# A delta-rule attention kernel with a gated MLP: scaling and turning in one operation, later joins, moves on ScalarE's queue

## The chip, the cores and the metric

One core of a Trainium2 chip runs one program: a linear attention with the delta rule, then a two-layer MLP with SiLU. The metric is the device time in microseconds. The kernel before took 643.09 us, the median of three runs (639.18 to 647.69).

## The reference

The inputs are q, k, v of shape (4 batches, 8 heads, 768 tokens, 48) in float32, beta of shape (4, 8, 768), and two weight matrices of 384 x 2048 and 2048 x 384.

```python
k_n = k / (np.linalg.norm(k, axis=-1, keepdims=True) + 1e-06)
state = np.zeros((B, H, D, D))
for t in range(S):
    y[:, :, t] = np.einsum('bhd,bhde->bhe', q[:, :, t], state)
    v_old = np.einsum('bhde,bhd->bhe', state, kt)
    state = state + bt * np.einsum('bhd,bhe->bhde', kt, vt - v_old)
x = y.transpose(0, 2, 1, 3).reshape(3072, 384)
h = x @ w_in
out = (h * (1.0 / (1.0 + np.exp(-h)))) @ w_out
```

## The kernel before

The 768 tokens are cut into six chunks of 128 (numbered 0 to 5), each chunk into two halves of 64 tokens, each half into two blocks of 32. Batches 0 and 1 form group 0 (`G0`), batches 2 and 3 group 1 (`G1`). Inside a chunk the recurrence over tokens is a unit triangular system for each of the 32 (batch, head) pairs. The kernel inverts it, and then needs the running `state` only at the borders of halves.

The stages for one chunk `c`, with the names that the profile shows:

- **Norms.** `lengths(c)` squares the keys (`square`, L409 to L426: tile `sq`, or `z` for chunks above 2, where the room of `z` is borrowed), sums them (`add_squares`, L427, tile `ss`) and runs `norm_steps` (L435): some twenty tiny VectorE operations that end in `spread` (the scale of each row, which feeds the matmul `pg` and its copy `step`) and `n_slot`, by which GpSimd scales the values `vf` (`size`, L521).
- **Scores.** `prepare(c)` turns the last keys and queries with VectorE's stream transpose (`turn_all`, L542, tile `kq`) and multiplies keys by keys and queries for each of the four batches (`score`, matmuls `pa` at L583). For each batch ScalarE copies one product out (`ap<-pa`, L598) and VectorE masks the other (L593). The PSUM room `A` has three banks that are handed out in turn; in this stretch the order of users is `pyc` of group 0, `pyc` of group 1, `pg`, then `pa` of batches 0, 1, 2, 3. So batch 2's scores take the bank of `pg` and wait for ScalarE's copy `step<-pg` (L504), and batch 3's take batch 0's bank and wait for its copies and masks. The 32 x 32 diagonal blocks go through DRAM (`blocks<-ap`, `g<-blocks`) so that each partition holds one block.
- **Inversion.** `invert(c)` (L678) does 31 steps of two VectorE operations each (`rank`, L689, and `x`, L694). It then scales `x` by `step` (L697), turns the lower rows' blocks into `g` (`turn_rows`: a quarter by GpSimd, L604, three quarters by VectorE, L601), and sends `g` and `x` through DRAM (`low<-g`, `up<-x`) to come back transposed as `xe`, `xi` and `crosses`.
- **Joins.** `merge` (L828, matmuls `py` and `px` at L843) joins blocks of 32 to triangles of 64. The first of them needs `xe<-low`.
- **Solve.** `solve(c)` takes the joins, then for each half: `keys` (`ph`, L889, which VectorE adds to `vf` at L894), `inner` (`pz`, L901, copied by ScalarE to `z`), `old` and `new` (`pyc`, L969 and L982) and `update` (`pu`, L921, added to `state` at L928). `even_heads` writes the half's outputs into `xT`, the MLP's transposed input. ScalarE copies the odd heads to `part` first, then copies twelve strips of even heads into `xT`. The odd heads cross partitions by five DMAs, `xT<-part`, issued by `move`.
- **MLP.** `feed_forward(c)`: chunk 1 uses plain products (`hidden`, `phid`, L1110), chunks 2 to 5 use seven products in place of eight (`hidden_by_products`, `hx` and `hu`, L1164, with sums of weights made once by `sum_w_in`, L1140, and sums of inputs made by `sum_x`, L1152). `combine` (`px` and `py`, L1330) does the second layer in the same way; ScalarE and VectorE collect its pieces (`o` at L1368 to L1374, `kept` at L1338, `o<-o,kept` at L1341).

**What sets the order.** `pin` fixes the order of instructions on each compute engine as the program issues them. `in_line` does the same for DMAs of SyncE's queue. A DMA on that queue waits for its data in place, and those behind it wait too. `linked` and `deep(..., n)` add waits: with `deep` and n = 3 each DMA of a load waits until the third one before it has landed. `run(n)` issues n pieces of the MLP of the chunk before (a piece is a handful of matmuls), and the main loop mixes pieces with stages of the chunk in hand: `go(steps, n)` advances a generator by n steps. So the MLP's matmuls are the filler that TensorE runs while a chunk's chain is with other engines. `paced` spreads the inversion of chunks 3 to 5 over the 44 items of `hidden_by_products`. Chunk 2's inversion is spread by a credit (L1800 to L1809), and four more pieces are run between its end and its joins (L1816).

`load_blocks(src, c, bs)` brings a group's keys or queries of a chunk in 32-row blocks, by six DMAs. Its rooms are the MLP's `gT`, or `ap`, or (for chunk 2) rooms of weight sums. The room `ap` takes first G0's keys and then G1's queries, so the latter wait until VectorE has turned the former.

Of the kernel before, what the change touches and what calls it, by code (L numbers as in the profile page):

```python
# [19 lines left out]
def kernel(  # L20
# [388 lines left out]
    def square(c, b):  # L409
# [12 lines left out]
        if (c, b) == (0, 3):  # L422
            pin(nc.scalar.activation(out=squared[c, b], in_=kb, func=ACTF.Square))
        else:
            pin(nc.gpsimd.tensor_tensor(out=squared[c, b], in0=kb, in1=kb, op=ALU.mult))
# [252 lines left out]
    def invert(c, step):  # L678
# [3 lines left out]
        def turn_rows(engine, s):  # L682
            engine(g[EVEN, :, s], x[EVEN, s, :].rearrange("p s t -> p t s"))

        for m in range(T - 1, 0, -1):
# [11 lines left out]
        pin(nc.vector.tensor_tensor(  # L697
            out=x, in0=x, in1=step[:].unsqueeze(2).to_broadcast([P, T, T]), op=ALU.mult
        ))
        for _ in range(1):  # L700
            yield
        if c == 1:
            put_up(x)
            return
        turn_rows(by_pool, slice(0, T // 4))
        turn_rows(by_dve, slice(T // 4, T))
        low, up = (tc.dram_tile([n, T, T], FP32, name=f"{name}{c}") for name, n in (("low", W), ("up", P)))
        issue(low[:], g[EVEN])
        issue(up[:], x)
# [250 lines left out]
    def move():  # L960
        for to, of in moves:
            in_line(nc.sync.dma_start(out=to, in_=of))
        moves.clear()
# [60 lines left out]
    def made(c, hf):  # L1024

        together(update(c, 0, hf), update(c, 1, hf))
        together(new(c, 0, hf), new(c, 1, hf))
        move()
        copy_out()
# [7 lines left out]
    def solve(c):  # L1037
# [34 lines left out]
        for hf in range(2):  # L1072
# [14 lines left out]
            copy_out()  # L1087
            if hf == 0:
                yield
# [712 lines left out]
    while left:  # L1802
        spent[0] = 0.0
        run()
        credit += 1.31 - spent[0]
        while left and credit > 0.0:
            left = next(steps, 0) != 0
            credit -= 0.38 + 0.00225 * m * (T - m) if m > 0 else 1.2
            m -= 1  # L1809
        if m == T - 6:  # L1810
            load_k(3)
    deep(load_blocks, k, 3, G1, n=3)
# [3 lines left out]
    for n in range(4):  # L1816
        run()
        go(after, (1, 1, 1, 0)[n])

    for c in range(2, NCH):  # L1820
        solving, more = solve(c), c + 1 < NCH
        for n in range(8):
            go(solving)
            run((1, 1, 2, 2, 1, 1, 2, 2)[n] if c == 2 else (2, 2, 2, 2, 1, 1, 2, 2)[n])
            if n == 2 and c > 2 and more:
                assert done[0] >= start(c) - OUTPUT - 4
                deep(load_blocks, k, c + 1, G1, n=3)
            if n == (1 if c == 2 else 3) and more:
                deep(load_blocks, q, c + 1, G0, n=3)
            if n > 2:  # L1830
                go(after, 8)
            if n == 5 and c == 2:
                go(sums_in, 2)
# [10 lines left out]
        go(prepare(c + 1))  # L1844
        linked(load_v, c + 1)
# [42 lines left out]
```

## Time and profile before

| | |
|---|---|
| Times of three runs | 643.09, 647.69, 639.18 us |
| The profiled execution's own time | 644.67 us |
| Its span, first to last instruction | 642.9 us (the rest, 1.8 us, lies around it) |
| Mean granted TensorE clock | 0.978 |
| TensorE busy | 615.2 us |
| VectorE / ScalarE / GpSimd busy | 445.9 / 239.2 / 100.5 us |
| DMA moved | 55.06 MB, mean 86 GB/s |

TensorE is busy or waiting; its idle time is 27.7 us in all (642.9 less 615.2). About 11.2 us of that lie in the first 180 us, where chunks 0 and 1 are begun, and 3.6 us at the end, after the last matmul. A row of the timeline has the start, the length, the engine, line and operation, out<-in with shapes, the count of merged instructions, and in brackets the idle time of the engine before it and what ended that. The profile counts two matmuls for each one of the program, since float32 takes two. A row with an engine's name and a "q" (SPq, ACTq) is the sequencer of that engine issuing a DMA.

### The profile page before, as it was taken

Reading aid. Unit: us, or ns where it says so; the run is one execution under the profiler, and the core shown is the slowest. Engines: PE = TensorE matmul, PEld = TensorE weight load, DVE = VectorE, ACT = ScalarE, POOL = GpSimd, SP = SyncE. Lnnn points to the kernel's source line nnn. Section 1 sums busy time; section 2 is a strip of 40 time slices with the busy share of each in tenths; the row PEclk is TensorE's granted clock in tenths of the full one; section 3 lists DMA queues with packets and bytes.
Section 4 is the critical chain, followed back from the end, with each engine's and each line's share of the span. In section 5 each row is a group of like instructions: output and inputs, shape, how many; then the busy total and the mean of one; then the engine's idle time right before and its main releaser. Section 6 shows DMA issues by size and latency. Waiting matters only on the chain.

```text
span 642.9 us, 21912 instructions
## 1 busy us (share of the span) xinstructions
PE 615.2 (96%) x9570; PEld 538.5 (84%) x9570; DVE 445.9 (69%) x946; ACT 239.2 (37%) x542; POOL 100.5 (16%) x99
## 2 busy tenths in 40 slices
PE   8889999999989969999999999999999999999997
PEld 5677788666779948898898988898998899988997
DVE  5855879998897953969884959895969965131332
ACT  3665665152251113434322434324434314434211
POOL 5442531245000040000050000050000020000000
PEclk9968999999999979999999999999999999999999
DMA  7755654165326166235073436074441060110011
GB/s 153 181 120 166 187 130 99 57 164 131 86 47 131 27 113 126 64 80 118 0 141 76 108 79 123 1 145 91 100 98 44 1 108 16 39 26 0 1 26 24
DMA packets 143935, 55.06 MB, mean 86 GB/s; under 512 B 113488, under 2 KB 137296, under 8 KB 143840
## 3 DMA queue, kind: packets, MB, share of 16 engines
q1 hardware_dynamic: 143360, 53.00, 37.1%
q8 instruction: 75, 1.23, 0.9%
q10 hardware_dynamic: 480, 0.67, 0.4%
q14 instruction: 20, 0.16, 0.1%
HBM read 40.99 MB, written 10.49 MB: 80 GB/s over the span
## 4 chain that ended last, share of the span: by engine, by line
PE 78%; DVE 10%; DMA 7%; issue 2%; SPq 1%; ACT 1%; POOL 1%; DVEq 0%; POOLq 0%
PE hu L1164 12%; PE px L1330 11%; PE hx L1164 10%; PE phid L1110 10%; PE py L1330 10%; PE po L1253 7%; PE pa L583 3%; PE pz L901 2%; DVE rank L689 2%; DVE x L694 2%; PE ph L889 1%; PE pyc L969 1%; DMA gT<-in_k_dram 1%; PE pu L921 1%; DMA gT<-in_q_dram 1%
## 5 line engine op out<-in xcount | busy, mean ns | idle before, releaser
L1110 PE MATMUL phid<-xT,w_in 128*128 128x256 f32 x384 | 92.6, 394 | 0.8 <-issue 0.7
L1110 PEld LDWEIGHTS phid<-xT,w_in 128*128 128x128 f32 x384 | 72.4, 194 | 12.0 <-issue 1.6
L1330 PE MATMUL py<-w_out,sums_of_g 128*128 128x192 f32 x320 | 57.6, 329 | 1.7 <-issue 1.5
L1330 PE MATMUL px<-sums_of_w,sums_of_g 128*128 128x192 f32 x320 | 56.8, 328 | 0.0
L1330 PEld LDWEIGHTS py<-w_out,sums_of_g 128*128 128x128 f32 x320 | 52.2, 190 | 2.7 <-issue 2.1
L689 DVE SCALAR_TENSOR_TENSOR rank<-g,step,x 128x31 f32<-128x31 f32 (+15 forms) x124 | 49.6, 400 | 5.9 <-DMA g<-blocks 3.0
L1330 PEld LDWEIGHTS px<-sums_of_w,sums_of_g 128*128 128x128 f32 x320 | 52.3, 190 | 0.5
L1310 DVE TENSOR_TENSOR sums_of_g<-gT 128x512 f32<-128x512 f32 (+2 forms) x44 | 33.5, 797 | 25.0 <-PE py L1330 18.8
L1164 PE MATMUL hx<-xT,w_in 128*128 128x256 f32 x192 | 48.0, 379 | 0.0
L694 DVE TENSOR_TENSOR x<-x,rank 128x31 f32<-128x31 f32 (+15 forms) x124 | 42.5, 342 | 4.4
L1164 PE MATMUL hu<-xT,w_in 128*128 128x256 f32 x192 | 45.4, 379 | 0.0
L1179 DVE TENSOR_TENSOR gT<-gT,hx 128x512 f32<-128x512 f32 x32 | 21.9, 685 | 31.4 <-PE hx L1164 30.7
L1341 DVE TENSOR_TENSOR o<-o,kept 128x192 f32<-128x192 f32 (+1 forms) x29 | 12.4, 427 | 42.2 <-ACT kept L1338 42.2
L1164 PEld LDWEIGHTS hu<-xT,w_in 128*128 128x128 f32 x192 | 36.5, 190 | 5.0
L1164 PEld LDWEIGHTS hx<-xT,w_in 128*128 128x128 f32 x192 | 36.4, 190 | 4.8
L604 POOL COPY g<-x 64x256 f32<-64x256 f32 x4 | 5.0, 1255 | 179.7 <-DVE x L697 179.7
L598 ACT COPY xT<-pyc 48x128 f32<-48x128 f32 (+2 forms) x120 | 31.1, 259 | 1.6
L928 DVE TENSOR_TENSOR state<-state,pu 48x384 f32<-48x384 f32 x44 | 24.2, 551 | 9.1 <-PE pu L921 8.1
L598 ACT COPY gT<-hu 128x512 f32<-128x512 f32 x32 | 18.7, 585 | 30.6 <-PE hu L1164 30.6
L901 PEld LDWEIGHTS pz<-vf,xi 64*64 64x64 f32 x768 | 25.5, 142 | 4.9 <-DVE vf L894 2.4
L1164 PE MATMUL hu<-sums_of_g,w_in 128*128 128x256 f32 x128 | 28.9, 379 | 0.0
L901 PE MATMUL pz<-vf,xi 64*64 64x48 f32 x768 | 27.4, 226 | 1.5 <-DVE vf L894 1.5
(234 smaller groups left out, 1203.9 us busy)
## 6 DMA issues: line engine op xcount, KB each, us to landing
vf<-in_v_dram SPq DMA_DIRECT2D x48, 96.0 KB, 2.8
out_dram<-o SPq DMA_DIRECT2D x42, 96.0 KB, 2.2
w_out<-in_moe_w_in_dram SPq DMA_DIRECT2D x12, 256.0 KB, 3.4
sums_of_w<-in_moe_w_out_dram SPq DMA_DIRECT2D x8, 384.0 KB, 3.7
blocks<-ap SPq DMA_DIRECT2D x40, 64.0 KB, 1.9
g<-blocks SPq DMA_DIRECT2D x4, 512.0 KB, 3.5
up<-x SPq DMA_DIRECT2D x4, 512.0 KB, 4.2
xi<-up SPq DMA_DIRECT2D x16, 128.0 KB, 3.7
```

Of the source, the lines that this page charges most:

```text
L583: pin(nc.tensor.matmul(pa[e][half, p * n * W : (p + 1) * n * W], lhsT=kq[rows, p, 0, half], rhs=kq[rows, p, js[0] : js[-1] + 1, half], sta ...
L598: return pin(nc.scalar.copy(to, of))
L689: pin(nc.vector.scalar_tensor_tensor(out=tv, in0=g[:, 0:m, m : m + 1].to_broadcast([P, m, n]), scalar=step[:, m : m + 1], in1=x[:, m : m + ...
L694: yield pin(nc.vector.tensor_tensor(out=x[:, 0:m, m:T], in0=x[:, 0:m, m:T], in1=tv, op=ALU.add))
L901: yield pin(nc.tensor.matmul(pz[rows, n * D : (n + 1) * D], lhsT=xis[g][rows, u * H + 2 * p + e, :], rhs=vfs[c][rows, hf, g * HB + u, p, : ...
L928: pin(nc.vector.tensor_tensor(out=to, in0=to, in1=by_heads(pu[of]), op=ALU.add))
L1110: pin(nc.tensor.matmul(ph[:, j * GT : (j + 1) * GT], lhsT=w_in[:, a, (2 * f + j) * P : (2 * f + j + 1) * P], rhs=xTs[c, hf][:, a, :], star ...
L1164: pin(nc.tensor.matmul(to[:, GT * i : GT * (i + 1)], lhsT=weights[:, f], rhs=moving, start=start and i == 0, stop=True, skip_group_check=True,
L1179: return lambda: pin(nc.vector.tensor_tensor(out=at(fs, j, hf), in0=at(fs, j, hf), in1=of(room), op=ALU.add))
L1253: pin(nc.tensor.matmul(pos[i][:, 0:DM], lhsT=hidden_of(0, hf, f // 2)[:, at : at + C], rhs=w_outs[f // HFF][:, f % HFF, :], start=(f == 0) ...
L1310: pin(nc.vector.tensor_tensor(out=sums_of_g[:, k, fs], in0=of[0], in1=of[1], op=op))
L1330: pin(nc.tensor.matmul(to, lhsT=at, rhs=quarter(f, *b) if isinstance(b, tuple) else sums_of_w[b][:, f], start=start and n == 0, stop=n == ...
```

## The change

Six things change. In the inversion of chunks 2 to 5 the lower rows are scaled and turned by one VectorE operation that writes `g` in transposed order; then the whole of `x` is scaled in place. The separate turn by GpSimd and VectorE goes. After chunk 2's inversion seven runs of pieces stand in place of four before the joins. One step of the generator goes too, and the credit takes nothing for the last step, so the joins stand six matmuls of the program (12 records) of `phid` later in TensorE's order. The odd heads' DMAs of chunks 2 to 5 are issued by ScalarE, after the second group's even heads, and leave SyncE's queue. The squares for chunks 3 to 5 are made by ScalarE in place of GpSimd. The steps of `lengths` for chunk 3 (and by their order those for 4 and 5) are issued earlier in the solve, ahead of the state's update. The last steps of `sum_w_in` come after chunk 3's scores. The loads of key and query blocks that ran under `deep` run without it, and the queries of chunks 4 and 5 for G0 are issued one stage later.

```diff
-        if (c, b) == (0, 3):
+        if c > 2 or (c, b) == (0, 3):
             pin(nc.scalar.activation(out=squared[c, b], in_=kb, func=ACTF.Square))
...
-        def turn_rows(engine, s):
-            engine(g[EVEN, :, s], x[EVEN, s, :].rearrange("p s t -> p t s"))
-
...
-        pin(nc.vector.tensor_tensor(
-            out=x, in0=x, in1=step[:].unsqueeze(2).to_broadcast([P, T, T]), op=ALU.mult
-        ))
-        for _ in range(1):
+        def scale(rows, to):
+            pin(nc.vector.tensor_tensor(
+                out=to, in0=x[rows], in1=step[rows].unsqueeze(2).to_broadcast([rows.stop - rows.start, T, T]),
+                op=ALU.mult,
+            ))
+
+        if c == 1:
+            scale(ALL_ROWS, x)
             yield
-        if c == 1:
             put_up(x)
             return
-        turn_rows(by_pool, slice(0, T // 4))
-        turn_rows(by_dve, slice(T // 4, T))
+        scale(EVEN, g[EVEN].rearrange("p t s -> p s t"))
         issue(low[:], g[EVEN])
+        scale(ALL_ROWS, x)
         issue(up[:], x)
...
-    def move():
+    def move(by_scalar=False):
         for to, of in moves:
-            in_line(nc.sync.dma_start(out=to, in_=of))
+            issue(to, of, by_scalar)
...
         together(new(c, 0, hf), new(c, 1, hf))
-        move()
+        if c == 1:
+            move()
         copy_out()
...
             copy_out()
+            move(True)
...
-            credit -= 0.38 + 0.00225 * m * (T - m) if m > 0 else 1.2
+            credit -= 0.38 + 0.00225 * m * (T - m) if m > 0 else 0.0
...
-    deep(load_blocks, k, 3, G1, n=3)
+    load_blocks(k, 3, G1)
...
-    for n in range(4):
+    for n in range(7):
         run()
-        go(after, (1, 1, 1, 0)[n])
+        go(after, int(n < 3))
...
-                deep(load_blocks, k, c + 1, G1, n=3)
-            if n == (1 if c == 2 else 3) and more:
-                deep(load_blocks, q, c + 1, G0, n=3)
-            if n > 2:
+                load_blocks(k, c + 1, G1)
+            if n == (1 if c == 2 else 4) and more:
+                load_blocks(q, c + 1, G0)
+            if n > 0:
                 go(after, 8)
-            if n == 5 and c == 2:
-                go(sums_in, 2)
...
         go(prepare(c + 1))
+        go(sums_in)
+        go(sums_in)
```

In the order of the built programs the following stands around chunk 2's scores. ScalarE, before: six strips, `o<-px`, `step<-pg`, eight copies `ap<-pa`. After: six strips, five DMAs `xT<-part`, `kept<-py`, `step<-pg`, eight copies `ap<-pa`. VectorE, before: `kq<-ap` (batches 2 and 3), eight masks. After: `o<-o,kept`, then `kq<-ap`, eight masks. Around chunk 3's and 4's scores only the five DMAs are new, between the last strip and `o<-px`, `step<-pg`.

## The prediction

> **What bounds the kernel now.** I read the page first, for who is busy and what the chain of waits is made of.
>
> ```profile
> span 642.9 us, 21912 instructions
> ...
> PE 615.2 (96%) x9570; PEld 538.5 (84%) x9570; DVE 445.9 (69%) x946; ACT 239.2 (37%) x542; POOL 100.5 (16%) x99
> ...
> PE 78%; DVE 10%; DMA 7%; issue 2%; SPq 1%; ACT 1%; POOL 1%; DVEq 0%; POOLq 0%
> ```
>
> TensorE is the bound, and the change leaves its matmuls alone. It can only gain where TensorE stands still, and lose where it makes TensorE stand still. So next I went through TensorE's timeline for idle time after chunk 1, where the change acts.
>
> ```profile
> 235.02 0.32 PE L843 MATMUL py<-xe,ap 32*32 32x32 f32 x4 [5.31 <-DMA xe<-low]
> 236.17 1.92 PE L843 MATMUL py<-xe,ap 32*32 32x32 f32 x124 [0.83 <-DMA xe<-low]
> 238.01 2.93 PE L1110 MATMUL phid<-xT,w_in 128*128 128x256 f32 x6
> ...
> 263.19 0.25 PE L901 MATMUL pz<-vf,xi 64*64 64x48 f32 x1 [1.02 <-DVE vf L894]
> ...
> 372.91 1.10 PE L583 MATMUL pa<-kq 48*64 48x128 f32 x32 [1.21 <-DVE kq L542]
> 374.27 1.43 PE L583 MATMUL pa<-kq 48*64 48x128 f32 x32 [0.26 <-DVE ap L593]
> ...
> 453.72 0.25 PE L901 MATMUL pz<-vf,xi 64*64 64x48 f32 x1 [0.47 <-DVE vf L894]
> ...
> 521.54 1.25 PE L843 MATMUL py<-xe,ap 32*32 32x32 f32 x124 [0.31 <-DMA xe<-low]
> ```
>
> The brackets are the prize: 5.31 + 0.83 = 6.14 us at chunk 2's joins, 1.02 + 0.47 us for `vf`, 1.47 us at chunk 3's scores, 0.31 us at chunk 5's joins, 9.4 us in all. The third view is the granted clock (PEclk, behind the engines' columns) in windows of time.
>
> ```profile
> 54.90:58.30 3.40, 3.40 (x12) 2.73 (x11) 0.00 (x0) 1.87 (x3) 1.84 (x1) 0.50 0.38 131
> 177.70:181.20 3.50, 2.27 (x39) 1.81 (x37) 3.43 (x6) 3.35 (x13) 0.00 (x0) 1.00 0.12 31
> 235.00:242.60 7.60, 6.75 (x198) 5.54 (x198) 3.27 (x6) 1.75 (x3) 0.41 (x1) 0.50 0.84 128
> ```
>
> After the wait at the joins TensorE runs at half clock for 7.6 us. The 124 `py` take 1.92 us there against 1.25 us at chunk 5.
>
> **Part by part.** First the joins. The chain of waits shows the path into them, and what six records of `phid` cost at full clock.
>
> ```profile
> 226.71 1.24 DVE x L697
> 228.06 1.25 POOL g L604
> 229.32 3.33 DMA low<-g
> 233.09 3.03 DMA xe<-low
> ...
> 240.94 1.84 PE ph L889 x64
> ...
> 245.50 2.79 PE phid L1110 x12
> ...
> 525.59 1.16 PE ph L889 x63
> ```
>
> The scaled turn does in one step of VectorE what L697 and L604 do in two, so `low` leaves at about 227.97 in place of 229.32, 1.35 us sooner. I cost the new step, 64x1024 with a transposed write, like L697, which has as many elements per partition (1.24 us). The turn that it replaces is the nearest row for the access pattern:
>
> ```profile
> 227.97 0.84 DVE L601 COPY g<-x 64x768 f32<-64x768 f32 x1
> ```
>
> Scaled to 1024 elements that is 1.12 us, with the stride on the reading side; no row has it on the writing side. I keep from 1.12 to twice 1.24 us. The Trainium skill, "SBUF — State Buffer", "Door 1: The DMA port swizzle", says that an access which crosses into a new 16-byte line each time pays a penalty, which speaks against this step; row L601 reads in such strides and pays none, and writing is shown by no run here. The scaling of `x` for `up` comes 1.24 us behind, so `up` leaves at about 229.25 against 229.8: nothing lost.
>
> TensorE gets 12 more records of `phid` before the joins, 2.79 us. Idle time left: 6.14 − 1.35 − 2.79 = 2.00 us, so 4.14 us are gained. The 12 records are missing later, between chunk 2's scores and its products, where nothing waits for TensorE to be slow. Half clock cost 0.67 us on `py`, 1.53 us on `phid` (2.93 against half of 2.79) and 0.7 us on `ph` (1.84 against 1.16), 2.9 us together. Whether it goes is open: the window at 177.7 us, with 1.2 us of idle time in it, kept the clock at 1.00, but at 54.9 us the clock was lost without a long wait. I take half, 1.4 us, with 0 and 2.9 as ends. The other three inversions save the same 1.35 us; only chunk 5's joins wait, so 0.31 us there.
>
> Norms sooner: VectorE's queue around 263.19.
>
> ```profile
> 254.65 2.30 DVE L928 TENSOR_TENSOR state<-state,pu 48x384 f32<-48x384 f32 x4 [5.91 <-PE pu L921]
> ...
> 261.27 1.28 DVE L1140 TENSOR_TENSOR w_in<-w_in 128x512 f32<-128x512 f32 x2
> 262.58 1.02 DVE L894 TENSOR_TENSOR vf<-vf,ph 128x384 f32<-128x384 f32 x2
> ```
>
> Between `state` and `vf` stand 5.6 us of norms and sums. They move into the 5.91 us of idle time before `state` or behind the scores, so `vf` comes when `ph` does, and 1.02 us go; in chunk 4 0.47 us go the same way. Sum 1.5 us, between 0.5 and 2.
>
> Squares on ScalarE: the kernel has one already.
>
> ```profile
> 8.69 0.52 ACT L423 ACTIVATE sq<-gT 128x384 f32<-128x384 f32 x1 [0.27 <-DMA gT<-in_k_dram]
> ```
>
> Four of these for each of three chunks stand beside TensorE's filler. I cost them at nothing: ScalarE is idle 63% of the span. Were that cover gone, the price would be 2.1 us a chunk. Loads without `deep` and a shorter SyncE queue let G1's queries land sooner, which would end chunk 3's 1.47 us. They can also crowd the `xi` transfers after the joins; I bound that by 0 to 1 us and take 0.
>
> Now what the DMAs on ScalarE's queue cost.
>
> ```profile
> L962 SPq DMA_DIRECT2D xT<-part x55: 597/607/1432, 89.5 to 557.1; - x55
> ...
> 91.64 0.37 ACTq L102 DMA_DIRECT2D g<-blocks  x1
> 92.06 0.60 ACT L1118 ACTIVATE gT<-phid 128x512 f32<-128x512 f32 x1 [0.92 <-DMA xT<-part]
> ```
>
> An issue holds SyncE's sequencer for 0.61 us, so five take 3.0 us, 3.2 us with the gaps. Row 91.64 shows that ScalarE computes nothing while its sequencer issues. The DMAs read `part`, which is written before the strips, so some of the issuing can run while the last strips are still being worked off: ScalarE stands still for between 0 and 3.2 us. I take 2.2 us, as the only row of such an issue has it wholly exposed. What is queued behind it, in chunk 2:
>
> ```profile
> 272.99 1.61 ACT L598 COPY xT<-pyc 48x128 f32<-48x128 f32 x6
> 274.63 0.33 ACT L1374 ACTIVATE o<-px 128x192 f32<-128x192 f32 x1
> ...
> 272.88 2.04 DVE L542 STREAM_TRANSPOSE kq<-ap 128x512 f32<-128x512 f32 x2
> 275.55 3.38 DVE L593 TENSOR_TENSOR ap<-pa,above 128x256 f32<-128x256 f32 x8 [0.62 <-ACT ap L598]
> 280.91 0.36 DVE L1341 TENSOR_TENSOR o<-o,kept 128x192 f32<-128x192 f32 x1 [0.72 <-ACT kept L1338]
> ...
> 273.99 3.72 PE L583 MATMUL pa<-kq 48*64 48x128 f32 x128
> ```
>
> Behind it stand `kept<-py`, then `step<-pg` (whose bank batch 2's scores take), and on VectorE `o<-o,kept` ahead of `kq<-ap`. The strips end at 274.6, the DMAs at 276.8, `kept` at 277.15, `o` (0.36) at 277.5, the first `kq` (1.02) at 278.6. Batch 2's scores, ready at 273.99 + 1.86 = 275.85, wait 2.8 us. Batch 3's wait for masks behind the second `kq`, 0.5 to 1 us. Sum 3.8 us; with nothing exposed 1.6 us are left by VectorE's new order, with 3.2 us exposed 4.8 us. Chunks 3, 4 and 5:
>
> ```profile
> 367.29 3.25 ACT L598 COPY xT<-pyc 48x128 f32<-48x128 f32 x12
> ...
> 463.52 1.61 ACT L598 COPY xT<-pyc 48x128 f32<-48x128 f32 x6
> 464.52 4.05 PE L583 MATMUL pa<-kq 48*64 48x128 f32 x128
> ...
> 557.75 0.33 ACT L1374 ACTIVATE o<-px 128x192 f32<-128x192 f32 x1
> 559.48 2.76 PE L1330 MATMUL px<-sums_of_w,sums_of_g 128*128 128x192 f32 x16
> ```
>
> In chunk 4 `step` ends at 465.13 + 2.2 + 0.5 = 467.85, and batch 2's scores, ready at 466.55, wait 1.3 us. In chunk 3 the strips end at 370.54, so `step` ends at 373.25, where batch 2 began at 372.91, so the 1.47 us are not gained but change hands: 0. In chunk 5 `o<-px` ends at 560.25, and the `px` of 559.48 that adds to what it reads waits 0.75 us.
>
> **The sum.** −4.14 − 1.4 − 0.31 − 1.5 + 3.8 + 1.3 + 0 + 0.75 = −1.5 us. The profiled execution took 644.67 us (642.9 and 1.8 around it); that gives 643.2 us, and on the median of 643.09 us, 1.6 us below it, **641.5 us**. What is gained at the joins is given back at the scores. Own range of this case, with the ends of the clock, of the exposure and a run's noise: 637 to 647.
>
> **Rivals.** *The issue is hidden* (nearly all of it runs while strips are worked off). Then the scores cost 1.6 us, chunk 3's 1.47 us are gained, and the clock stays up: −4.14 − 2.9 − 0.31 − 2 − 1.47 + 1.6 = −9.2 us, 634 us. For it: `part` is long written when the strips end. Against it: the exposed issue of row 91.64.
>
> *ScalarE's queue becomes the bound at the scores.* If all 3.2 us are exposed, the waits are 4.8, 1.0, 2.3 and 1.75 us, 9.9 us in place of 5.85. A wait of 3 to 4 us in the middle of small `pa` matmuls then halves the clock as at 235 us, where it was low for 10.2 us (7.6 us, and 2.6 us before it); dense work loses half of that, 5.1 us a time. One such loss gives 643.09 − 1.5 + 4.0 + 5.1 = 650.7 us, two 655.8. It decides from some 2.5 us of wait on. For it: 5.31 us idle lost the clock. Against it: the window at 177.7 us, where a wait of 1.2 us lost nothing. The Trainium skill, "TensorE: Matmul & The Clock Gate", Part 1, says that one idle window of about 3.4 us halves the clock; by that rule chunk 2's 2.8 us would just not, and the row at 54.9 us, lost without so long a pause, says that less can do.
>
> *The strided write costs double* (2.5 us). `low` leaves no sooner, and the joins gain only 2.79 us: 643.2 us.
>
> **Chances.** Forecast 0.5, issue hidden 0.2, ScalarE's queue 0.2, strided write 0.1. The range 633 to 651 reaches to the hidden issue and to one loss of clock. Two per cent is 12.9 us, about what a measurement of this kernel can tell from no change. To be faster by that, the hidden issue would need nearly every bracket above and more: 0.07. To be slower by that, it takes two losses of clock: 0.1. Within: 0.83.
>
> **What would show it.** In the new profile: `py<-xe,ap` of chunk 2 with some 2 us of idle time before it in place of 6.14, low clock shorter or gone after it; ACTq rows `xT<-part` of 0.6 us with ScalarE idle some 2 us behind the last strips; idle time before `pa` in chunks 2 and 4, released by `kq` or by `step`; none before `pz`. The prediction is wrong if the ACTq issues lie under the strips, if TensorE waits for `xi`, or if the clock falls between 275 and 300 us.

## The result, and the profile after

The changed kernel took 666.11 us, the median of four runs (663.57 to 672.81), beside 643.71 us for the kernel before on the same chip. The ratio is 1.0366, with a 95% interval of 1.0261 to 1.0471: slower. The prediction was 641.5 us, with a range from 633 to 651.

The profiled execution took 667.58 us with a span of 665.9 us, 23.0 us more than before. The page gives busy times and shares, and then the group of the scores' matmuls (busy time, mean ns of one, idle time ahead of them and what ended most of it).

```profile
span 665.9 us, 21881 instructions
...
PE 626.5 (94%) x9570; PEld 548.8 (82%) x9570; DVE 448.1 (67%) x946; ACT 243.8 (37%) x554; POOL 82.5 (12%) x83
...
L583 PE MATMUL pa<-kq 48*64 48x128 f32 (+1 forms) x768 | 29.4, 311 | 19.4 <-DVE kq L542 16.6
```

TensorE has the same 9570 records, but is busy for 11.3 us longer (626.5 against 615.2): the same matmuls at a lower clock. It is also idle for 11.7 us longer (39.4 against 27.7). The scores waited 16.6 us for VectorE's `kq`.

TensorE's timeline shows where. The brackets hold the idle time before a row.

```profile
217.85 4.10 PE L1332 MATMUL px<-sums_of_w,sums_of_g 128*128 128x192 f32 x16 [2.16 <-DVE sums_of_g L1312]
...
239.83 0.25 PE L843 MATMUL py<-xe,ap 32*32 32x32 f32 x4 [0.62 <-DMA xe<-low]
240.76 1.25 PE L843 MATMUL py<-xe,ap 32*32 32x32 f32 x124 [0.68 <-DMA xe<-low]
...
274.44 2.05 PE L583 MATMUL pa<-kq 48*64 48x128 f32 x64
282.53 3.69 PE L583 MATMUL pa<-kq 48*64 48x128 f32 x64 [6.04 <-DVE kq L542]
...
384.09 2.20 PE L583 MATMUL pa<-kq 48*64 48x128 f32 x36 [5.13 <-DVE kq L542]
...
478.42 3.78 PE L583 MATMUL pa<-kq 48*64 48x128 f32 x64 [2.10 <-DVE kq L542]
485.54 3.69 PE L583 MATMUL pa<-kq 48*64 48x128 f32 x64 [3.34 <-DVE kq L542]
```

Chunk 2's joins wait 1.30 us where they waited 6.14. The scores of chunks 2, 3 and 4 now wait 6.04, 5.13 and 5.44 us, and a group of 64 `pa` takes 3.69 us there, nearly twice the 2.05 us of the group in front at full clock. The view by windows gives the clock in the column before the last two.

```profile
280.70:287.50 6.80, 4.97 (x68) 4.67 (x69) 5.00 (x11) 2.59 (x8) 0.14 (x1) 0.50 0.24 41
...
478.70:492.30 13.60, 10.26 (x138) 9.48 (x130) 9.95 (x19) 3.00 (x10) 1.10 (x2) 0.50 0.48 91
```

The stages, from the starts and ends of the `pa` and `py<-xe,ap` rows in the two timelines:

| Stage | before | after | difference |
|---|---|---|---|
| Start to the end of chunk 1's scores | 188.8 | 192.1 | +3.3 |
| to chunk 2's joins | 46.2 | 47.7 | +1.5 |
| chunk 2's joins to the end of its scores | 42.7 | 46.4 | +3.7 |
| to chunk 3's joins | 53.7 | 52.0 | −1.7 |
| chunk 3's joins to the end of its scores | 44.3 | 49.6 | +5.3 |
| to chunk 4's joins | 51.1 | 52.3 | +1.2 |
| chunk 4's joins to the end of its scores | 41.8 | 49.1 | +7.3 |
| to chunk 5's joins | 52.4 | 55.0 | +2.6 |
| to the end | 121.9 | 121.6 | −0.3 |

Three solves hold 16.3 of the 23.0 us. The first row's 3.3 us are no effect of the change. Up to there every engine has the same instructions in the same order, and TensorE waits the same 1.2 and 0.5 us at chunk 1's scores. What differs is the clock (before, then after):

```profile
178.00:188.50 10.50, 8.74 (x148) 7.39 (x150) 9.16 (x17) 6.59 (x22) 1.13 (x2) 1.00 0.23 44
```

```profile
178.00:188.50 10.50, 8.73 (x81) 7.04 (x80) 8.24 (x16) 5.55 (x19) 1.13 (x2) 0.68 0.23 44
```

So below, beside whole times, stands the time from the end of chunk 1's scores to the end of the profile, where the kernels differ: 454.1 us before, 473.8 after.

**What the scores wait for.** The chain of waits of the changed kernel runs through chunk 2's scores like this:

```profile
275.02 0.60 ACTq L102
275.62 0.04 issue
275.66 2.89 DMA xT<-part
278.57 2.56 DMA ap<-in_q_dram
...
281.31 1.09 DVE kq L542
282.40 0.14 issue
282.53 3.69 PE pa L583 x64
```

A load of the next chunk's queries, `ap<-in_q`, starts only when a move of odd heads, `xT<-part`, has landed. They share no data. In the next two blocks, SyncE's queue shows the loads being held (start, time until the last of six is issued); the kernel before stands below.

```profile
246.58 15.72 SPq L190 DMA_DIRECT2D ap<-in_k_dram  x6
262.61 6.06 SPq L190 DMA_DIRECT2D gT<-in_q_dram  x6
268.77 10.11 SPq L190 DMA_DIRECT2D ap<-in_q_dram  x6
```

```profile
244.00 2.86 SPq L190 DMA_DIRECT2D ap<-in_k_dram  x6
250.48 4.94 SPq L190 DMA_DIRECT2D gT<-in_q_dram  x6
...
265.64 2.71 SPq L190 DMA_DIRECT2D ap<-in_q_dram  x6
```

The view of waits says what ended them: over the whole of the changed kernel (total, times, longest), SyncE's sequencer waited

```profile
SPq L190 <- DMA xT<-part: 50.8, 15, 13.5
```

No such row of L190 is in the kernel before. The compiled program gives the reason. SyncE's and ScalarE's transfers share eight completion semaphores, handed out in turn in the order in which the framework's planner places them, whichever engine issues them. A transfer that takes over a semaphore waits until the one that had it last has landed. In the changed kernel the plan has the five moves of chunk 2's first half ahead of the sixth `ap<-in_k`:

```
SyncE    ap<-in_k (6th)  waits DMAHW1 <- ScalarE xT<-part (1st)
SyncE    gT<-in_q (1st)  waits DMAHW2 <- ScalarE xT<-part (2nd)
SyncE    gT<-in_q (2nd)  waits DMAHW3 <- ScalarE xT<-part (3rd)
```

So loads that had left SyncE's queue early now stand there until ScalarE's strips are done and its moves have landed. I call this theory L. Theory I is the one that the prediction priced: ScalarE's time for issuing. Theory O: the other parts of the change cost.

### The profile page after: what moved, and what is told of

It is laid out like the page before. It is cut to its first block, busy times and chain, and to the rows that moved or that the text cites. A ratio compares the mean times of both kernels' runs of the same rounds, so it can differ in the third digit from the quotient of the medians.

```text
span 665.9 us, 21881 instructions
## 1 busy us (share of the span) xinstructions
PE 626.5 (94%) x9570; PEld 548.8 (82%) x9570; DVE 448.1 (67%) x946; ACT 243.8 (37%) x554; POOL 82.5 (12%) x83
## 3 DMA queue, kind: packets, MB, share of 16 engines
q8 instruction: 75, 1.23, 0.8%
## 4 chain that ended last, share of the span: by engine, by line
PE 77%; DVE 10%; DMA 5%; ACT 3%; issue 2%; ACTq 1%; SPq 0%; POOL 0%; DVEq 0%; POOLq 0%
PE px L1332 12%; PE hu L1166 12%; PE hx L1166 10%; PE py L1332 10%; PE phid L1112 9%; PE po L1255 6%; PE pa L583 3%; DVE rank L686 2%; PE pz L901 2%; ACT xT L598 2%; DVE x L691 2%; DMA xT<-part 2%; PE ph L889 2%; PE pyc L982 1%; DVE kq L542 1%
## 5 line engine op out<-in xcount | busy, mean ns | idle before, releaser
L1332 PE MATMUL px<-sums_of_w,sums_of_g 128*128 128x192 f32 x320 | 59.1, 337 | 2.5 <-DVE sums_of_g L1312 2.2
L686 DVE SCALAR_TENSOR_TENSOR rank<-g,step,x 128x31 f32<-128x31 f32 (+15 forms) x124 | 54.1, 436 | 5.9 <-DMA g<-blocks 3.0
L1332 PEld LDWEIGHTS px<-sums_of_w,sums_of_g 128*128 128x128 f32 x320 | 53.8, 195 | 3.9 <-issue 2.8
L691 DVE TENSOR_TENSOR x<-x,rank 128x31 f32<-128x31 f32 (+15 forms) x124 | 46.0, 371 | 4.4
L583 PE MATMUL pa<-kq 48*64 48x128 f32 (+1 forms) x768 | 29.4, 311 | 19.4 <-DVE kq L542 16.6
L1312 DVE TENSOR_TENSOR sums_of_g<-gT 128x512 f32<-128x512 f32 (+2 forms) x44 | 27.7, 668 | 25.6 <-PE py L1332 18.8
L583 PEld LDWEIGHTS pa<-kq 48*64 48x64 f32 x768 | 25.5, 165 | 22.9 <-issue 19.0
L626 POOL MEMSET x<- 128x1024 f32 x4 | 3.8, 958 | 251.8 <-DMA ap<-in_q_dram 224.9
L1332 PE MATMUL py<-w_out,gT 128*128 128x192 f32 x160 | 31.3, 350 | 0.0
L1193 ACT ACTIVATE gT<-gT 128x1024 f32<-128x1024 f32 x16 | 16.9, 1054 | 36.6 <-DVE gT L1181 36.6
```

The source lines that it names most:

```text
L583: pin(nc.tensor.matmul(pa[e][half, p * n * W : (p + 1) * n * W], lhsT=kq[rows, p, 0, half], rhs=kq[rows, p, js[0] : js[-1] + 1, half], sta ...
L686: pin(nc.vector.scalar_tensor_tensor(out=tv, in0=g[:, 0:m, m : m + 1].to_broadcast([P, m, n]), scalar=step[:, m : m + 1], in1=x[:, m : m + ...
L691: yield pin(nc.vector.tensor_tensor(out=x[:, 0:m, m:T], in0=x[:, 0:m, m:T], in1=tv, op=ALU.add))
L1193: return lambda: pin(nc.scalar.activation(out=to, in_=to, func=ACTF.Silu, scale=scale))
L1312: pin(nc.vector.tensor_tensor(out=sums_of_g[:, k, fs], in0=of[0], in1=of[1], op=op))
L1332: pin(nc.tensor.matmul(to, lhsT=at, rhs=quarter(f, *b) if isinstance(b, tuple) else sums_of_w[b][:, f], start=start and n == 0, stop=n == ...
```

## The experiments

**moves_back**: the changed kernel, moves on SyncE again at their old place.

```diff
-        if c == 1:
-            move()
+        move()
         copy_out()
...
             copy_out()
-            move(True)
```

> The changed kernel with one part undone: the odd heads' pieces go through SyncE's queue again, from the place in made() where they stood before; the joins, the scaled turn, the squares, the norms and the loads stay as changed. Theory L (SyncE's loads of the next chunk's keys and queries stand behind ScalarE's moves, because each load waits for the completion semaphore that the move before it in the plan uses): 634 to 645 us; the queries ap<-in_q of chunk 2 are issued by 269 us and not up to 278.6, the waits of TensorE at pa<-kq in chunks 2, 3 and 4 fall from 6.04, 5.13 and 3.34 us to under 3 each, and the three halvings of the clock at 281, 383 and 479 us go. Theory I (the 3 us that ScalarE spends on issuing hold up the scores): also 634 to 650, since the issues leave ScalarE. Theory O (the loads' new places, the strided scale or the norms' new place are what costs): 655 us or more, and the queries still land after 275 us.

649.32 us, ratio 1.0103 (1.0023 to 1.0182). `ap<-in_q` of chunk 2 leaves from 264.32 us on, the waits at `pa` are 0.56 us in chunk 2, none above 0.35 in chunk 3 and 2.44 in chunk 4. Most of the loss goes with the moves, so O falls as the main cause. The time came out above L's range, though inside I's: something else costs too, in chunk 4.

**only_moves**: the kernel before with `move(True)` after the second `copy_out()` and the old `move()` for chunk 1 alone.

> The kernel before with one part of the change alone: from chunk 2 on the odd heads' pieces go through ScalarE's queue, after the second half's strips. Theory L: 655 to 675 us; SyncE's queries ap<-in_q of chunk 2 are issued until 275 us or later (268.4 in the kernel before), TensorE waits 4 to 7 us at pa<-kq in chunks 2, 3 and 4, and the clock halves there. Theory I: the same direction, but TensorE's waits at pa<-kq grow by about 2 us each, to 648 to 655 us, and end with ScalarE, not with a landing. Theory O: 640 to 648 us, as before.

670.0 us, ratio 1.0388 (1.0310 to 1.0466): this part alone costs 25 us, more than the whole change. In the window 240 to 284 us its waits show the loads, and its timeline the scores:

```profile
SPq L190 <- DMA xT<-part: 18.6, 3, 11.0
```

```profile
284.38 3.69 PE L583 MATMUL pa<-kq 48*64 48x128 f32 x64 [6.93 <-DVE kq L542]
```

**issue_time**: the kernel moves_back, with ScalarE work in place of ScalarE issues.

```diff
             copy_out()
+            for _ in range(6):
+                by_act(pad[:], pad[:])
```

> The changed kernel with the moves on SyncE's queue again, and at the place on ScalarE where they were issued six copies of a 128x192 tile of its own (some 0.33 us each, 2.0 us in all, as much as the changed kernel's issues reach beyond the strips: strips' end 275.02 to kept 276.97 us). It adds work that the reference doesn't need. Theory L: at most 2 us each in chunks 2, 3 and 4 above the kernel with the moves back, so 0 to 6 us over it and under 650; SyncE's queries are as early as there. Theory I: 655 us or more, TensorE's waits at pa<-kq back at 5 to 6 us. Theory O: within 2 us of the kernel with the moves back.

654.88 us, ratio 1.0163 (1.0083 to 1.0242). The six copies took 2.26 us, chunk 2's scores waited 2.79 us and lost the clock for 6.83 us. Against moves_back that is some 4 us by the ratios, with overlapping intervals: ScalarE's time matters, but it is a fraction of 22 us. The absolute bound (under 650) was missed with moves_back's own.

**sync_late**: the moves at their new place in the program, issued by SyncE (`move()` for `move(True)`).

> The changed kernel with the moves at their new place in the program, after the second half's strips, but issued by SyncE. Place and queue were changed together; this takes them apart. Theory L: within 1% of the kernel with the moves at the old place (634 to 648 us), since the plan puts them at the same place in SyncE's queue, ahead of ap<-in_q, and nothing waits for another queue's transfer. Theory I: the same. Theory O, and a theory that the later place itself costs: 655 us or more.

647.41 us, ratio 1.0012 (0.9956 to 1.0067), 451.0 us from chunk 1's scores on. The queue costs, the place doesn't: between this kernel and the changed one, which differ in the issuing engine alone, lie 22.8 us by the ratios.

**loads_first**: the changed kernel, same moves on ScalarE at the same place, the planner's order held.

```diff
         if by_scalar:
-            pin(nc.scalar.dma_start(out=to, in_=of))
+            behind(pin(nc.scalar.dma_start(out=to, in_=of)), line[-1])
```

> The changed kernel, moves on ScalarE's queue and at their new place, with one word more for the plan: a move may stand there only behind the last of SyncE's loads issued so far. ScalarE issues the same transfers at the same place in its order; what differs is which transfer's completion semaphore each load and each move takes over: the next chunk's keys and first queries no longer wait for a move, and the moves wait for loads instead. Theory L (the shared semaphores): the six ap<-in_q of chunk 2 are issued by 271 us (278.6 in the changed kernel, 268.4 before), TensorE's waits at pa<-kq in chunks 2, 3 and 4 fall from 6.04, 5.13 and 3.34 us to under 3 us, 645 to 655 us. Theory I (ScalarE's time for issuing, or the moves' later landing): 660 us or more, waits unchanged.

657.21 us, ratio 1.0205 (1.0150 to 1.0261), between the ranges of L and I; waits at `pa` 2.62, 0.20 and 0.57 us; `ap<-in_q` from 271.34 us on. The built programs have the same instructions in the same order on every engine and differ only in semaphores and in the waits on them, and 9 us went. The edit had a flaw: it also held the first loads of the program that ScalarE issues, which changed their semaphores, and chunk 0's scores began at 17.9 us in place of 13.3. The next four runs deal with that.

**moves_first**: the same edit on only_moves, where the queries' loads stand ahead of the outputs.

> The kernel before with the moves alone on ScalarE's queue, and the plan's order held so that a move stands only behind the loads issued so far: the same edit as in the changed kernel's own test, on a kernel where the queries' loads stand ahead of the outputs. With the moves alone, and the plan free, it was 670.0 us. Theory L: most of those 26 us are the loads' waits for moves; TensorE's wait at pa<-kq in chunk 2 falls from 6.93 to 2 to 3.5 us (ScalarE's issues alone: kept, then o on VectorE, then kq), those of chunks 3 and 4 from 4.86 and 3.37 to under 3; 648 to 657 us, so ScalarE's issues with the clock that they cost are worth 4 to 13 us and the shared semaphores 13 to 22. Theory I (the issues alone): 662 us or more.

652.55 us, ratio 1.0148 (1.0089 to 1.0206), 17 us under only_moves; waits at `pa` 1.76, 0.52 and 0.99 us, now for `step`; 455.7 us from chunk 1's scores on.

**moves_first_again**: the same kernel once more.

> The kernel before with the moves on ScalarE's queue behind the loads, once more with more rounds. In its first profile 5.8 of the 7.4 us above the kernel before lay ahead of 195 us, where both run the same instructions in the same order; from there to the end it took 455.7 us against 454.1. If that first part was chance, the time comes out 2 to 5 us above the kernel before (ratio 1.003 to 1.008) and the stage from chunk 1's scores on at 454 to 459 us; if ScalarE's issues cost what the whole times said, 1.010 to 1.020 again, and the stage at 460 us or more.

654.68 us, 1.0143 (1.0093 to 1.0194), and 456.4 us from chunk 1's scores on. So both: the whole time stayed, and the stage is only 2 us longer than before. Chunk 0's scores began at 17.7 us again, 4.4 us late, so most of the rest was the shifted start and not chance.

**moves_behind**: the order held for the moves alone (on only_moves).

```diff
         for to, of in moves:
-            issue(to, of, by_scalar)
+            done = issue(to, of, by_scalar)
+            if by_scalar:
+                behind(done, line[-1])
```

> As the two runs of the kernel before with the moves on ScalarE behind the loads, with the plan's order held for the moves alone: in those runs it was held for every transfer that ScalarE issues, the first loads of the program among them, whose semaphores changed, and the first scores began at 17.3 and 17.7 us where all other kernels have 12.9 to 13.5. Expected: first scores at 13.5 us, 646 to 650 us, 2 to 6 us above the kernel before (ScalarE's issues alone: waits at pa<-kq of 1.8, 0.7 and 1.0 us); if the 10 us above stay, the issues cost them in a place that I have not seen.

648.87 us, ratio 1.0061 (1.0031 to 1.0092): 3.9 us above the kernel before, of the 25 that the same moves cost with the plan left free. Scores from 13.4 us on, 455.4 us from chunk 1's scores to the end, no row of L190 that waits for `xT<-part`. ScalarE and TensorE in chunk 2:

```profile
270.57 0.53 ACT L598 COPY xT<-pyc 32x128 f32<-32x128 f32 x2
271.51 1.92 ACTq L102 DMA_DIRECT2D xT<-part  x3
273.48 0.33 ACT L1378 ACTIVATE o<-px 128x192 f32<-128x192 f32 x1 [2.38 <-PE pa L583]
273.71 0.18 ACT L504 COPY step<-pg 128x32 f32<-128x32 f32 x1
```

```profile
273.94 2.17 PE L583 MATMUL pa<-kq 48*64 48x128 f32 x64 [1.44 <-ACT step L504]
```

This is theory I by itself: two of the five issues run beside the last strips (unlike the one of the prediction's row 91.64), three do not. ScalarE stands still for 2.38 us, `step` comes late, the scores wait 1.44 us (0.69 and 0.98 in chunks 3 and 4) and keep the clock. The built program differs from that of only_moves in semaphores and waits alone, as above. The profile is of the fastest run, 643.70 us. Its stage is 1.3 us longer than the 454.1 us of the kernel before, although its clock was low at the joins for 6.83 us in place of 10.24, which is worth 1.7 us; together that is near the 3.9 us of the medians.

**loads_ahead**: the same edit on the changed kernel.

> The changed kernel with the order held for the moves alone. Expected: 4 us under its first form (657.2), 650 to 655 us, first scores at 13.5 us, the rest as there: TensorE's wait of 2.6 us at pa<-kq in chunk 2, and of 2.9 us at pu<-z,kb in chunk 4, where ScalarE's moves wait for queries that stand behind the outputs. If it stays at 657 us or more, the shift of the start was not a cost.

655.17 us, ratio 1.0140 (1.0090 to 1.0189), just above the 655 expected; scores from 13.6 us on. By the ratios 14.6 us of the changed kernel's loss went. Chunk 2's scores waited 2.52 us and lost the clock for 6.83 us. In chunk 4 the dependency bites the other way: the plan now has the queries first, and ScalarE's moves wait for them in place.

```profile
459.12 6.41 ACTq L102 DMA_DIRECT2D xT<-part  x5
465.57 0.48 ACT L598 COPY z<-pz 128x384 f32<-128x384 f32 x1 [9.22 <-DMA xT<-part]
```

TensorE waits 3.05 us there, at `pu`. Holding the order mends the loads and, where the loads themselves are late, hands the wait to ScalarE.

**only_joins**: the kernel before with the joins three pieces later.

```diff
-    for n in range(4):
+    for n in range(7):
         run()
-        go(after, (1, 1, 1, 0)[n])
+        go(after, int(n < 3))
```

> The kernel before with one part alone: chunk 2's joins behind seven pieces of the feed-forward after the inversion and not four. Theory J (the prediction's step): TensorE's idle time ahead of the joins falls from 6.14 us to 2.8 to 3.6, and the halving of the clock at 232 us goes or loses half its 10.24 us; 637 to 643 us, some 3 to 5 under the kernel before. Rival (the three pieces are only missed later, where the scores or the second half lack them): the idle time falls there and comes back as waits of chunk 2, 643 to 647 us.

638.53 us, ratio 0.9915 (0.9884 to 0.9946), 449.0 us from chunk 1's scores on. The joins' waits, for 5.31 and 0.83:

```profile
234.02 0.25 PE L843 MATMUL py<-xe,ap 32*32 32x32 f32 x4 [1.45 <-DMA xe<-low]
235.12 1.25 PE L843 MATMUL py<-xe,ap 32*32 32x32 f32 x124 [0.85 <-DMA xe<-low]
```

This part is a gain, 5 us, and nothing lacks the three pieces later. It moves the joins further than the change does: without the change's credit the three pieces are nine matmuls of the program, and in the change they are six. That can be why the wait fell below the expected 2.8 to 3.6 us.

Why did sync_late, which has later joins too, gain nothing? Two more costs show in its profile. The first is in the inversion, where two operations of VectorE take 1.71 and 1.67 us. It is in the changed kernel as well, which the rows show (VectorE's timeline, then GpSimd's, then VectorE's of the kernel before):

```profile
206.25 1.84 DVE L1312 TENSOR_TENSOR sums_of_g<-gT 128x384 f32<-128x384 f32 x1
208.12 0.56 DVE L1312 TENSOR_TENSOR sums_of_g<-sums_of_g,gT 128x384 f32<-128x384 f32 x1
...
209.39 1.66 DVE L686 SCALAR_TENSOR_TENSOR rank<-g,step,x 128x220 f32<-128x220 f32 x1
```

```profile
206.20 1.47 POOL L521 TENSOR_TENSOR vf<-vf,n_slot 128x768 f32<-128x768 f32 x1 [21.39 <-DVE rank L686]
209.34 1.47 POOL L521 TENSOR_TENSOR vf<-vf,n_slot 128x768 f32<-128x768 f32 x1 [1.66 <-DMA vf<-in_v_dram]
```

```profile
203.02 0.55 DVE L1310 TENSOR_TENSOR sums_of_g<-gT 128x384 f32<-128x384 f32 x1
...
204.87 0.44 DVE L689 SCALAR_TENSOR_TENSOR rank<-g,step,x 128x220 f32<-128x220 f32 x1
```

Operations that take 0.55 and 0.44 us in the kernel before take 1.84 and 1.66 while GpSimd scales `vf`. Before, the scaling stood behind GpSimd's quarter of the turn and ran at 229 us, with VectorE idle. The second cost is in chunk 4's solve: in sync_late SyncE's queue issues the next queries behind the outputs, and waited 9.0 us for those.

```profile
SPq L104 <- DVE o L1343: 9.0, 1, 9.0
```

**size_after** holds GpSimd's scalings until `x` is scaled (on sync_late).

```diff
-        pin(nc.gpsimd.tensor_tensor(out=vf, in0=vf, in1=of, op=ALU.mult))
+        sized = pin(nc.gpsimd.tensor_tensor(out=vf, in0=vf, in1=of, op=ALU.mult))
+        if c in scaled:
+            behind(sized, scaled[c], Sync)
```

> The kernel with the late moves on SyncE's queue, with GpSimd's two scalings of vf held until x is scaled, as they stood before behind GpSimd's quarter of the turn. Theory P (two VectorE operations of 0.4 to 0.6 us take 1.7 to 1.9 while GpSimd scales vf inside the inversion, 1.2 us lost each, since the turn that stood ahead of them in GpSimd's order is gone): no such long operations, TensorE's wait at px near 220 us falls from 2.18 to under 0.9 us with no halving of the clock there, low leaves some 2 us sooner against the inversion's start; the waits for vf at pz of up to 1.0 us come back; 640 to 647 us, 1 to 4 us under the kernel without the hold where both start alike. Rival (the long operations are loading of instructions or chance): they stay, and the time is within 1 us.

644.94 us, ratio 1.0012 (0.9975 to 1.0049), the same ratio as sync_late. The long operations and the wait at `px` are gone, as theory P says, and the inversion ends sooner. But the joins then wait 2.30 us in place of 1.18, with the clock low for 10.24 us. In sync_late, in loads_n3 and in the changed kernel TensorE lost the clock for 3.41 us at `px`, came to the joins late and waited only 1.2 to 1.3 us; every other kernel with later joins waits 2.3 to 2.5 us. The mechanism is shown, a gain in the whole time isn't.

**turn_back** has the old turn on sync_late, the diff's scaled turn undone.

> The kernel with the late moves on SyncE's queue and the old turn: x scaled whole, then turned by GpSimd (a quarter) and VectorE (the rest). Theory P: GpSimd's scalings of vf stand behind the turn again, so no VectorE operation of 1.7 us inside the inversion and TensorE's wait at px falls from 2.18 to under 0.9 us; low leaves 2.6 us after the inversion's end and not 2.0, so the idle time ahead of the joins is 0.6 us longer in chunk 2, and under 1 us in the later chunks; 641 to 648 us, equal to or up to 2 us under the kernel with the scaled turn. Theory S (the scaled turn itself brings the 1.35 us that was predicted, each chunk): slower by 1 to 4 us than that kernel.

645.46 us, ratio 1.0015 (0.9977 to 1.0052). No long operation in the inversion and no wait at `px`; the time is the same as with the scaled turn. So the whole time doesn't bear out theory S. It doesn't show the turn to be worth nothing either, since this kernel has the old credit too, and with it nine matmuls ahead of the joins and not six (see joins_turn).

**loads_n3** issues the queries of chunks 4 and 5 where they were (`n == 3`, on sync_late).

> The kernel with the late moves on SyncE's queue, with the first queries' loads of chunks 4 and 5 issued one piece sooner, where they stood before (after the fourth and not the fifth step of the chunk). Theory Q (at the later place they stand behind four transfers of outputs in SyncE's queue, which wait for the outputs: in chunk 4 gT<-in_q was issued from 452.9 us on and not from 436.6 as with the joins alone): gT<-in_q of chunk 4 leaves 10 us or more sooner, VectorE's wait of 3.9 us at kq<-gT goes, TensorE's waits at pa<-kq of 1.79 and 0.88 us and the half clock at 467 go; 640 to 645 us, 3 to 5 under the kernel without this. Rival R (what delays chunk 4's scores is ScalarE's own work, the squares it took over): waits unchanged, 645 to 649 us.

643.34 us, ratio 0.9995 (0.9964 to 1.0026). Chunk 4's queries leave 14 us sooner, of which 4 us are a faster start of this profile. Sync_late first, then loads_n3, in SyncE's queue:

```profile
452.94 2.96 SPq L190 DMA_DIRECT2D gT<-in_q_dram  x6
```

```profile
439.10 3.96 SPq L190 DMA_DIRECT2D gT<-in_q_dram  x6
...
448.37 3.90 SPq L104 DMA_DIRECT2D out_dram<-o  x4
```

VectorE's wait of 3.9 us at `kq<-gT` is gone and TensorE's two waits at `pa` (1.79 and 0.88) are 1.17 and 0.22, with no half clock there. So theory Q's mechanism is shown, but not its gain: the 4 us between the medians lie within the scatter, and from chunk 1's scores on the profile took 451.8 us, 0.8 more than sync_late's.

**hold_and_loads**: the changed kernel with moves on SyncE, scalings held, loads as before.

> The changed kernel with three things mended: the moves on SyncE's queue, GpSimd's scalings of vf held until x is scaled, the loads as before. What stays of the change: the scaled turn, the joins three pieces later, the squares by ScalarE, the norms sooner. If the causes found so far (shared semaphores and ScalarE's issues, GpSimd beside VectorE, the queries behind the outputs) are all, 636 to 641 us, at or up to 3 us under the kernel with the later joins alone (638.5); if the squares or the norms cost as well, 642 us or more.

641.50 us, ratio 0.9964 (0.9931 to 0.9997), half a microsecond above the range; 447.5 us from chunk 1's scores on, 1.5 below only_joins. Chunk 4's four batches of scores run without a gap. The squares on ScalarE and the norms' new place, which it keeps, show no cost there.

**joins_turn** and **joins_again**: only_joins with the scaled turn and held scalings, and only_joins once more beside it.

> The kernel before with two parts of the change: the joins three pieces later, and the scaled turn with GpSimd's scalings of vf held until x is scaled. Theory T (the scaled turn is worth what the rows show, low leaving 2.0 us after the inversion's end and not 2.6): idle time ahead of chunk 2's joins 0.6 us shorter than the 2.30 us with the later joins alone, the time 0 to 1.5 us under that kernel's, 636 to 639 us. Rival U (what keeps the mended kernel 3 us above the one with the later joins alone is the scaled turn or the held scalings): 640 to 643 us.

> The kernel before with the later joins alone once more, on the same chip as the kernel that adds the scaled turn, so that the two are compared side by side. Expected: 637 to 640 us, under the kernel before by 0.6 to 1.1%, as the first time; if it comes out at 641 us or more, the 3 us between it and the mended kernel were the chip's.

640.58 us, 0.9920 (0.9887 to 0.9953), and 640.25 us, 0.9947 (0.9907 to 0.9988). By its time joins_turn misses T's range and lies in U's, but the later joins alone came out the same beside it, so neither the turn nor the held scalings show a cost. The joins wait 2.51 us with the scaled turn and 2.42 without, not 0.6 less. The two kernels differ in one thing more: joins_turn has the change's credit, so its joins stand six matmuls later than in the kernel before, and those of joins_again nine. The three matmuls between are 1.4 us of filler, half of the prediction's 2.79. The path from the inversion's last step to the first join shows the turn without the filler (only_joins, then joins_turn):

```profile
225.46 0.19 DVE L694 TENSOR_TENSOR x<-x,rank 128x31 f32<-128x31 f32 x1
```

```profile
232.60 0.19 DVE L693 TENSOR_TENSOR x<-x,rank 128x31 f32<-128x31 f32 x1
...
240.18 0.25 PE L845 MATMUL py<-xe,ap 32*32 32x32 f32 x4 [1.77 <-DMA xe<-low]
```

From the end of that step to the first `py` it is 8.37 us in only_joins (`py` at 234.02 above) and 7.39 in joins_turn. In all eight profiles with the old turn it is 8.2 to 8.5 us, in all ten with the scaled turn 7.2 to 7.5. So the scaled turn gains 1.0 us on this path, the three matmuls that come with it take that back, and the whole time shows nothing. Three kernels beat the kernel before by 0.4 to 0.9%: the later joins alone, the later joins with the scaled turn and held scalings, and hold_and_loads.

## Why the prediction was wrong

**The step that failed** is "Loads without `deep` and a shorter SyncE queue let G1's queries land sooner". I took the moves' leaving SyncE's queue as freeing the loads behind them. They came to stand behind the moves more than before, through the shared semaphores: 50.8 us of waits in fifteen loads. No term of the sum and no rival had this. With the plan left free the moves cost 25 us (only_moves), with the loads planned ahead 3.9 us (moves_behind), so some 21 us are this, the clock that the waits lost among them. In the changed kernel planning the loads ahead took off 14.6 us.

**ScalarE's issues** were priced at 3.8, 1.3, 0 and 0.75 us, 5.85 in all, from 2.2 us exposed. moves_behind has 2.38 us exposed in chunk 2, waits of 1.44, 0.69, 0.98 and 0.34 us, 3.45 in all, and 3.9 us (2.0 to 5.9) on the whole time. The mechanism and the releaser (`step`) were right. The changed kernel with the loads ahead (loads_ahead), which has the VectorE order that was priced, waited 2.83, 0.57, 1.31 and 0.35 us in chunks 2 to 5 for the forecast 3.8, 0, 1.3 and 0.75: 5.06 us for 5.85, so the size was near. Missed was the clock: the forecast let chunk 2's 2.8 us keep it, but 2.52 us in loads_ahead and 2.79 us in issue_time lost it for 6.83 us each. In the eighteen profiles each wait of TensorE of 2.1 us or more behind 200 us went with a low clock, while of those of 1.2 to 2.0 us some did and some did not; at chunk 2's scores 1.44 to 1.90 us kept it (moves_behind, moves_first and its repeat).

**The rival of the clock** (650.7 with one loss, 655.8 with two) priced a loss at 5.1 us, half of 10.2 us. Waits of 2 to 6 us at the scores did halve the clock, for 6.83 us in chunks 2 and 3 and 13.65 us in chunk 4, so the losses were 3.4, 3.4 and 6.8 us. Its condition, all 3.2 us exposed, did not occur: ScalarE stood still for 1.94 us in chunk 2. In the changed kernel the waits came from the loads. The Trainium skill, "TensorE: Matmul & The Clock Gate", Part 1, has the clock halved by one idle window of about 3.4 us that runs free of the kernel's start. The traces fit a window that runs free: the low stretches inside the spans are 3.41 us long or multiples of it, and chunk 1's waits of 1.2 and 0.5 us kept the clock before and lost it after. They don't fit a whole idle window as the condition, since 1.8 us in two pieces were enough there.

**The joins**: 4.14 us of waiting were to go, 2.79 by six matmuls and 1.35 by the scaled turn. With both, and no clock lost at `px`, 3.63 to 3.84 us went (joins_turn, hold_and_loads, size_after), so the step was right and somewhat high. The 4.84 us in the changed kernel are in part luck, since TensorE came late there; the 3.84 us of only_joins are nine matmuls, without the turn. Of the clock I took half. The low stretch of 10.24 us was 6.83 and 3.41 us in the two profiles of the later joins alone, 3.41 in joins_turn, 10.24 again in size_after and hold_and_loads, and none in issue_time and the changed kernel: with 2.3 to 2.5 us of waiting in all but the last it came out anywhere between all and nothing, so that half of it was a guess at the middle.

**The scaled turn** was costed at 1.24 us for the strided write, with 1.12 and 2.48 as ends. It took 1.97:

```profile
232.45 1.97 DVE L695 TENSOR_TENSOR g<-x,step 64x1024 f32<-64x1024 f32 x1
234.45 1.23 DVE L695 TENSOR_TENSOR x<-x,step 128x1024 f32<-128x1024 f32 x1
```

So `low` leaves 2.0 us after the inversion and not 1.24, against 2.6 before, and `xe<-low` is issued 3.0 us behind it and not 3.4: 1.0 us gained and not 1.35, between the forecast and the rival of the double cost, which had nothing. "SBUF — State Buffer", "Door 1: The DMA port swizzle" of the Trainium skill, spoke against this step, and the row bears it out.

**Left out**: that GpSimd's quarter of the turn kept its scalings of `vf` out of the inversion. I costed the turn's removal on VectorE and SyncE and never asked what stood behind it in GpSimd's order. It cost VectorE 1.3 and 1.2 us and TensorE 2.16 us at `px` in chunk 2. The 1.02 us at `pz` did go, but not by the norms' place as forecast: they are gone in only_joins too, where the norms stand as before. There the 0.47 us in chunk 4 stay, and in the changed kernel they are gone. Chunk 3's 1.47 us at the scores are none in only_joins and 0.71 in joins_again, so they hang on the later joins as well.

**Loads**: issuing the queries one stage later was costed at nothing. In chunk 4 it put them behind outputs that are late, 2.7 us of waiting in sync_late. The squares at nothing stand uncontradicted, though no run tried them alone.

## What to carry to other kernels

Moving a transfer to another engine's queue does not part it from the transfers left behind while they share completion semaphores: look up, for each load behind it in the plan, whose semaphore it takes over, and plan the early loads ahead of the late transfer or leave them in one queue. When an operation is taken off an engine, ask what was queued behind it and where that will now run. And in a kernel with a clock that drops on short waits, compare stages from the point where two kernels begin to differ before believing a few microseconds of the whole. When one part is tested by itself, see what filler stands ahead of the wait in both kernels: here three matmuls hid a gain of 1.0 us.

## What the runs showed of the hardware that was not expected

VectorE operations on two operands in SBUF took 1.84 and 1.66 us in place of 0.55 and 0.44 while a GpSimd operation of 1.47 us ran. The loss is nearly the other's whole length, as the Trainium skill says in "SBUF — State Buffer", "🔬 SBUF: two separate sides", of the port pair that the two engines lock in turn. A write in strides of 128 bytes cost 1.6 times the same product written in order (1.97 against 1.23 us, with half the partitions). And the same instructions around 180 us lost the clock for 3.41 or 6.83 us in ten of eighteen profiles, of kernels whose instructions don't differ up to there (three have other semaphores at their first loads). Half of 6.83 us is 3.4 us, 0.5% of the whole, so such losses can be part of why runs of one kernel lie up to 2% apart.
